# Holding back GpSimd's weight sums for the sixth and seventh output product of a Strassen-like layer

## The chip, the cores and the metric

One core of a Trainium2 chip. The metric is the device time of one execution in microseconds (us), median over runs. All runs quoted are in the fast state. Ratios are the mean time of one kernel's fast runs over that of the other's of the same rounds, so not quite the ratio of the medians quoted beside them.

## The reference, cut to what matters

```python
attn_out = _attn_ref(q, k, v, proj)          # hashed attention, 4 x 8 heads, 768 x 64
x = attn_out.transpose(0, 2, 1, 3).reshape(3072, 512)
h = x @ w_in                                 # 512 -> 2048
g = h * (1.0 / (1.0 + np.exp(-1.702 * h)))
return g @ w_out                             # 2048 -> 512: the part that matters here
```

## The kernel before

Both layers are computed with seven products in place of eight (a Strassen-like form with seven right-hand and left-hand sums), and in `g @ w_out` this is done twice, one form inside the other. So there are three blocks of tokens, each with seven *output products* (order `OUTER`), and each of these is made of seven *part products* on TensorE. An output product needs

- four sums of quarters of W_out (`inner_sums`), made on GpSimd (POOL) once, and used by all three blocks,
- four sums of quarters of g (`g_sums`: t1, a difference in place, t2, t4), made on VectorE for each output product during the one before it,
- additions of the part products on VectorE, and for some output products the accumulation onto an earlier one (`acc`).

In this kernel the operands lie in tiles of SBUF, and TensorE's products in tiles of PSUM.

```python
def sums_a(eng, a11, a12, s3, a22, s1, s2, s4, a21=None):
    a21 = s3 if a21 is None else a21
    return [lambda: eng.tensor_tensor(s1, a21, a22, op=Alu.add),
            lambda: eng.tensor_tensor(s3, a11, a21, op=Alu.subtract),
            lambda: eng.tensor_tensor(s2, s1, a11, op=Alu.subtract),
            lambda: eng.tensor_tensor(s4, a12, s2, op=Alu.subtract)]
# sums_b, used by g_sums on nc.vector: t1, b12 in place, t2, t4 (cut)
# ...
OUTER = (1, 2, 6, 7, 5, 3, 4)
# ...
def inner_sums(at):                  # at: place in OUTER; four sums of 128 x 512 on GpSimd
    # ... (at == 0 cut)
    return sums_a(nc.gpsimd, *w_quarters(OUTER[at])) if at < len(OUTER) else []
# ...
def product_of_halves(n, acc, after):
    # ... (cut)
    nc.scalar.copy(u, product(1))
    add(c11, product(2), u)
    if acc is not None:
        add(c11, c11, acc[:, 0])     # the accumulation of the first quarter
    nc.scalar.copy(c12, product(3))
    after(0)
    add(v, product(6), u)            # the fourth part product: the first that reads t2
    add(c21, product(7), v)
    if acc is not None:
        add(v, v, acc[:, 1])
        add(c22, c21, acc[:, 3])
        add(c21, c21, acc[:, 2])
    add(c12, c12, v)
    after(1)                         # t1 of the next output product
    # ... (product 5, after(2), product 4, after(3): the other g_sums of the next)
# ...
for n, (sb, o) in enumerate(steps_out):        # 21 output products
    # ... (fetch of the next g cut)
    for f in inner_sums(n + 4):                # GpSimd's sums for the fifth, sixth, seventh
        f()                                    # are issued in the first, second, third
    later_sums = g_sums(n + 1)
    # ... (cut)
    ms[o] = product_of_halves(n, None if acc is None else ms[acc], after)
```

The order on GpSimd is the order above, and nothing else makes these sums wait: GpSimd runs them as soon as it has done the work issued to it before, in the first layer (in the trace, from 642.6 us on).

Of the kernel before, what the change touches and what calls it, by code (L numbers as in the profile page):

```python
# [8 lines left out]
F32 = mybir.dt.float32  # L9
# [29 lines left out]
def kernel(  # L39
# [17 lines left out]
    nc = tc.nc  # L57
# [147 lines left out]
# [7 lines that stand above are left out]
# [458 lines left out]
    def feed_forward(tag, late=()):  # L670
# [8 lines left out]
        OUTER = (1, 2, 6, 7, 5, 3, 4)  # L679
        with ExitStack() as fctx:  # L680
# [62 lines left out]
            def w_quarters(o):  # L743

                w = wqs[LEFT[o]]
                x = [w[:, i, F4 * j : F4 * (j + 1), :] for i in range(2) for j in range(2)]
                at = OUTER.index(o)
                if at == 0:
                    return x[0:2] + rooms[3:4] + x[3:] + rooms[0:3]
                return x + rooms[3 * at + 1 : 3 * at + 4]  # L750

            def inner_sums(at):

                if at == 0:
                    w = w_quarters(OUTER[0])
                    return sums_a(nc.gpsimd, *w, wqs[LEFT[OUTER[0]]][:, 1, 0:F4, :])
                return sums_a(nc.gpsimd, *w_quarters(OUTER[at])) if at < len(OUTER) else []
# [4 lines left out]
            def fetch(n):  # L762
                sb, o = steps_out[n]
                for h in range(2):
                    cs = slice(h * F4, (h + 1) * F4)
                    loader[0].dma_start(out=raw_g[n % 2][:, cs], in_=g_dram[len(LEFT) * sb + RIGHT[o], :, cs, :])
# [14 lines left out]
            def g_sums(n):  # L781
                return sums_b(nc.vector, *g_quarters(n)) if n < len(steps_out) else [lambda: None] * 4
# [3 lines left out]
            def turned(c, i, j, q0, q1):  # L786

                for q in range(q0, q1):
                    h, k = divmod(q, 2)
                    y = ys[j].rearrange("p b (d r) -> p r b d", r=4)[:, 2 * i + h, k * (TH // 32) : (k + 1) * (TH // 32), :]  # L790
                    nc.vector.transpose(y, c[:, q].rearrange("p (b t) -> p b t", t=32))  # L791

            def written(sb, j, halves, queues):
                for b in halves:
                    blocks = slice(b * (TH // 32), (b + 1) * (TH // 32))
                    for a in range(4):
                        t0 = (2 * sb + j) * XT + b * TH
                        dst = out[t0 : t0 + TH, a * P : (a + 1) * P].rearrange("(b t) d -> t b d", t=32)
                        queues[a % len(queues)].dma_start(out=dst, in_=ys[j][32 * a : 32 * (a + 1), blocks, :])

            def product_of_halves(n, acc, after):

                sb, o = steps_out[n]
                wq, gq = w_quarters(o), g_quarters(n)
                m = wholes[n % len(wholes)]
                u, v = (gp.tile([P, TH], F32, tag=x, name=x, bufs=2) for x in ("u", "v"))
                c11, c12, c21, c22 = (m[:, i] for i in range(4))

                def product(i):
                    ps = bank()[:, 0:TH]  # L810
                    for c in range(F4):
                        nc.tensor.matmul(ps, wq[LEFT[i]][:, c, :], gq[RIGHT[i]][:, c, :], start=(c == 0), stop=(c == F4 - 1))  # L812
                    return ps

                def add(dst, x, y):
                    nc.vector.tensor_tensor(dst, x, y, op=Alu.add)  # L816
# [4 lines that stand above are left out]
                    add(c11, c11, acc[:, 0])  # L821
                nc.scalar.copy(c12, product(3))
                after(0)
                add(v, product(6), u)
# [6 lines that stand above are left out]
                after(1)  # L831
                p = product(5)
                add(c22, p, c21 if acc is None else c22)
                add(c12, p, c12)
                after(2)
                add(c21, product(4), c21)
                after(3)
                return m
# [14 lines left out]
            for sb in range(n1):  # L853
                for mt in range(MT):
                    n = sb * MT + mt
# [41 lines left out]
            st2 = fctx.enter_context(tc.tile_pool(name=f"st2{tag}", bufs=1, side="right"))  # L897
            ys.update({j: st2.tile([P, XT // 32, P], F32, name=f"y{j}") for j in range(2)})
            ms, pending = {}, []
            for n, (sb, o) in enumerate(steps_out):  # L900
                final = n + 1 == len(steps_out)
                if 0 < n and n + 1 < len(steps_out):
                    fetch(n + 1)
                for f in inner_sums(n + 4):
                    f()
                later_sums = g_sums(n + 1)
                m = wholes[n % len(wholes)]

                def after(at):
                    if at == 0:  # L910
                        while pending:
                            pending.pop(0)()

                    for f in later_sums[at : at + 1] if n == 0 else ([], later_sums[0:1], later_sums[1:2], later_sums[2:])[at]:
                        f()
                    if final and at == 2:
                        for q in (0, 1, 3):
                            turned(m, 1, 0, q, q + 1)
                        written(sb, 0, (1,), loader + [nc.scalar])
                    if final and at == 3:  # L920
                        turned(m, 1, 0, 2, 3)
                        written(sb, 0, (0,), loader + [nc.scalar])

                acc = {6: 1, 7: 6, 2: 1, 3: 6, 4: 7}.get(o)
                if o == 3:
                    pending.pop(0)()
                ms[o] = product_of_halves(n, None if acc is None else ms[acc], after)

                def flat(x):
                    return x.rearrange("p q t -> p (q t)")  # L930

                if o == 5:
                    m5, m6, m7 = (ms[i] for i in (5, 6, 7))
                    pending += [lambda a=m6, b=m5: nc.vector.tensor_tensor(flat(a), flat(a), flat(b), op=Alu.add),
                                lambda a=m5, b=m7: nc.vector.tensor_tensor(flat(a), flat(a), flat(b), op=Alu.add),
                                lambda a=m5: turned(a, 1, 1, 0, 4)]
                elif o in (2, 3):
                    pending.append(lambda a=ms[o], j=int(o == 3): turned(a, 0, j, 0, 4))
                    if o == 3:
                        pending.append(lambda sb=sb: written(sb, 1, (0, 1), loader))  # L940
                elif o == 4 and not final:
                    pending.append(lambda a=ms[4]: turned(a, 1, 0, 0, 4))
                    pending.append(lambda sb=sb: written(sb, 0, (0, 1), loader))
                yield

    def whole(steps):
        for _ in steps:
            pass

    ff = feed_forward("", in_chunks[len(in_chunks) - LATE :])  # L950
    attention(ff)
    whole(ff)
# [5 lines left out]
    with tc.If(unsafe, preferred_fallthrough_block=False):  # L958
        with tc.tile_pool(name="cv3", bufs=1) as cv:
            for x in in_chunks:  # L960
                whole(convert(cv, *x))
        for f in in_sums(0):
            f()
        shifted_attention()
        for f in sums_b(nc.vector, *quarters_x(0)):
            f()
        whole(feed_forward("2"))
# [27 lines left out]
```

## Time and profile before

| | kernel before |
|---|---|
| median of the first three runs | 895.95 us (895.92 to 897.0) |
| median of six runs, with those beside the changed kernel | 896.31 us |
| span of the profiled execution | 895.6 us, mean granted clock 0.993 |
| TensorE busy | 877.3 us (98%) |
| longest wait of TensorE | 3.8 us, for t2a in the third output product |
| that product, start to start | 19.07 us, where the fifth takes 12.09 |

(The granted clock is the share of TensorE's full clock that it was given; 1.00 is full.) Nearly all of the span TensorE is at work. A kernel like this is read by looking for the few places where it isn't: the list of TensorE's waits comes first, then the timeline of the engine that it waited for. The lines are in the prediction below.

### The profile page before, as it was taken

To read this page: it belongs to the slowest core of one execution; us is meant where nothing else is said; L and a number is where in the kernel's file an instruction comes from. 1 tells how busy PE (TensorE), PEld (TensorE's weight loads), DVE (VectorE), ACT (ScalarE), POOL (GpSimd) and SP (SyncE) were. 2 spreads that over 40 slices of the span, in tenths; PEclk is the share of its full clock that TensorE was granted. 3 is DMA by queue.
4 is the path that set the end of the run, shared out by engine and by line. 5 is a ranking of instruction groups with operands and counts; after the bars stand their busy time and mean duration, and the time that the engine had idled before them with its cause. 6 is when DMAs were issued, how large, how long until landed. Compare 5 with 4: busy or idle time off the path is not lost.

```text
span 895.6 us, 11963 instructions
## 1 busy us (share of the span) xinstructions
PE 877.3 (98%) x4077; PEld 507.2 (57%) x4077; DVE 710.9 (79%) x1020; ACT 313.3 (35%) x519; POOL 312.5 (35%) x273
## 2 busy tenths in 40 slices
PE   9999999999999999999999999999989999999995
PEld 5444444444444444444444444444868888888884
DVE  4598888888889954777777887888896977897785
ACT  5765666666665642223222222322000000000000
POOL 4243233222333263766433444659950000000000
PEclk9999999999999999999999999999989999999998
DMA  4644544556544103555456545575825565467524
GB/s 102 113 90 82 103 82 80 87 98 96 95 83 82 45 1 118 194 194 192 160 199 211 200 165 203 193 249 183 304 102 188 176 208 213 161 229 235 189 95 97
DMA packets 169477, 132.01 MB, mean 147 GB/s; under 512 B 123936, under 2 KB 138432, under 8 KB 164032
## 3 DMA queue, kind: packets, MB, share of 16 engines
q1 hardware_dynamic: 167712, 129.69, 50.7%
q10 hardware_dynamic: 1696, 1.48, 0.6%
q8 instruction: 34, 0.56, 0.3%
q14 instruction: 35, 0.29, 0.1%
HBM read 79.69 MB, written 50.33 MB: 145 GB/s over the span
## 4 chain that ended last, share of the span: by engine, by line
PE 94%; DVE 3%; DMA 1%; issue 1%; ACTq 0%; SPq 0%; ACT 0%; DVEq 0%
PE product L699 32%; PE product L812 27%; PE ps L429 16%; PE av L453 14%; PE dn L472 3%; PE hash L405 1%; DVE xT L816 1%; PE tp L363 1%; DMA q<-in_q_dram 1%; ACTq L417 0%; PE warm L356 0%; PE hash L370 0%; DVE y L791 0%; DVE acc L445 0%; DVE t2a L218 0%
## 5 line engine op out<-in xcount | busy, mean ns | idle before, releaser
L430 ACT ACTIVATE e<-ps 128x768 f32<-128x768 f32 x192 | 151.4, 812 | 19.2 <-PE ps L429 13.2
L429 PE MATMUL ps<-qT,kT 64*128 64x384 f32 x768 | 155.1, 482 | 0.0
L699 PE MATMUL product<-xT,w_in_sb 128*128 128x512 f32 x288 | 135.4, 592 | 0.0
L453 PE MATMUL av<-e,v 128*64 128x385 f32 x768 | 130.2, 486 | 0.9 <-ACT xT L466 0.9
L437 POOL TENSOR_TENSOR acc<-e 128x768 f32<-128x768 f32 x32 | 49.6, 1549 | 209.5 <-DVE acc L445 90.3
L707 ACT ACTIVATE c<-c 128x512 f32<-128x512 f32 x72 | 45.4, 630 | 186.6 <-issue 78.9
L453 PEld LDWEIGHTS av<-e,v 128*64 128x64 f32 x768 | 54.9, 136 | 70.6 <-issue 69.0
L699 PEld LDWEIGHTS product<-xT,w_in_sb 128*128 128x128 f32 x288 | 54.6, 190 | 68.5 <-issue 63.1
L699 PE MATMUL product<-t_x,s_in 128*128 128x512 f32 x192 | 90.2, 592 | 0.0
L429 PEld LDWEIGHTS ps<-qT,kT 64*128 64x128 f32 x768 | 68.2, 188 | 35.5 <-issue 35.5
L216 POOL TENSOR_TENSOR v<-c,u 128x512 f32<-128x512 f32 x24 | 34.1, 1422 | 129.4 <-ACT c L707 129.4
L818 ACT COPY u<-product 128x256 f32<-128x256 f32 x21 | 7.8, 372 | 173.4 <-PE product L812 131.8
L429 PE MATMUL ps<-qf,kf 64*128 64x384 bf16 x384 | 63.0, 324 | 0.7 <-ACT e L430 0.5
L699 PEld LDWEIGHTS product<-t_x,s_in 128*128 128x128 f32 x192 | 36.5, 190 | 45.9 <-issue 43.8
L438 POOL TENSOR_TENSOR acc<-acc,e 128x768 f32<-128x768 f32 x32 | 56.7, 1771 | 2.5
L699 PE MATMUL product<-xT,s_in 128*128 128x512 f32 x96 | 45.1, 592 | 0.0
L699 PE MATMUL product<-t_x,w_in_sb 128*128 128x512 f32 x96 | 45.1, 592 | 0.0
L429 PEld LDWEIGHTS <-kf 64*128 64x128 bf16 x384 | 18.9, 94 | 42.2 <-issue 20.7
L479 DVE STREAM_TRANSPOSE rt<-dn 128x384 f32<-128x384 f32 x32 | 18.6, 580 | 25.7 <-PE dn L472 25.6
L465 ACT COPY vs<-av 128x1 f32<-128x1 f32 x32 | 5.1, 159 | 95.1 <-PE av L453 95.0
L812 PE MATMUL product<-raw_g,xT 128*128 128x256 f32 x152 | 36.3, 388 | 0.0
L490 DVE TENSOR_TENSOR xT<-xT,rt 128x384 f32<-128x384 f32 x32 | 32.6, 1020 | 1.7
(200 smaller groups left out, 1569.6 us busy)
## 6 DMA issues: line engine op xcount, KB each, us to landing
raw_g<-g_dram SPq DMA_DIRECT2D x22, 1024.0 KB
s_in<-g_dram SPq DMA_DIRECT2D x20, 1024.0 KB
g_dram<-c SPq DMA_DIRECT2D x72, 256.0 KB
g_dram<-t SPq DMA_DIRECT2D x48, 256.0 KB
raw<-in_moe_w_out_dram SPq DMA_DIRECT2D x16, 512.0 KB
raw<-in_moe_w_in_dram SPq DMA_DIRECT2D x15, 512.0 KB
v<-in_v_dram SPq DMA_DIRECT2D x32, 192.0 KB
g_dram<-u SPq DMA_DIRECT2D x24, 256.0 KB
```

Source lines behind the costliest of these rows:

```text
L216: return [lambda: eng.tensor_tensor(t1, b12, b11, op=Alu.subtract), lambda: eng.tensor_tensor(b12, b22, b12, op=Alu.subtract), lambda: eng ...
L429: nc.tensor.matmul(ps[:, j, 0:HS], a[hs, keys], m[hs, cols], start=not last, stop=last)
L430: nc.scalar.activation(es[c][:, kt, :, 0:HS], ps[:, :, 0:HS], Act.Exp, scale=1.0 / D**0.5)
L437: nc.gpsimd.tensor_tensor(acc, es[c][:, 0, :, 0:HS], es[c][:, 1, :, 0:HS], op=Alu.add)
L438: nc.gpsimd.tensor_tensor(acc, acc, es[c][:, 2, :, 0:HS], op=Alu.add)
L453: nc.tensor.matmul(av[D * j : D * (j + 1), :], vt[:, t, j, :], es[c][:, t, j, :], start=(t == 0), stop=(t == T - 1))
L472: nc.tensor.matmul(dn[D * j : D * (j + 1), :], ones, acc[:, j, :], start=True, stop=True)
L479: nc.vector.transpose(rt, dn)
L490: nc.vector.tensor_tensor(x_of(n, c), x_of(n, c), rt.rearrange("p (t s) -> p t s", t=GT), op=Alu.mult)
L699: nc.tensor.matmul(ps, wq[LEFT[i]][:, kc, :], xq[RIGHT[i]][:, kc, :], start=(kc == 0), stop=(kc == K2 - 1))
L707: nc.scalar.activation(c, c, Act.Gelu_apprx_sigmoid)
L812: nc.tensor.matmul(ps, wq[LEFT[i]][:, c, :], gq[RIGHT[i]][:, c, :], start=(c == 0), stop=(c == F4 - 1))
```

## The change

In the kernel before, GpSimd's eight sums for the sixth and seventh output product run beside VectorE's sums in the second and third. They are not needed so early. In the changed kernel two copies of one element, each reading an element that VectorE writes, are put on GpSimd's queue ahead of them, so that they start later.

```diff
             ms, pending = {}, []
+            mark = st2.tile([1, 1], F32, name="mark")
             for n, (sb, o) in enumerate(steps_out):
                 ...
-                for f in inner_sums(n + 4):
+                if n in (3, 4):
+                    nc.gpsimd.tensor_copy(mark, ms[OUTER[n - 1]][0:1, 0, 0:1])
+                for f in inner_sums({0: 4, 3: 5, 4: 6}.get(n, len(OUTER))):
                     f()
```

`ms[OUTER[n - 1]][0:1, 0, 0:1]` is an element of c11 of the output product before. The copy waits for the last write to it, the accumulation `add(c11, c11, acc[:, 0])` of the third and of the fourth output product, which VectorE does about half way through them.

## The prediction

> **What bounds the kernel now.** I read the page first, then TensorE's waits over the whole run, then the timeline of TensorE, VectorE and GpSimd around the one long wait, then a table of stretches there. The page says that TensorE is nearly always busy (the first line below) and that GpSimd (POOL) has nothing to do after about three quarters of the span (the second, one digit per 22.4 us).
>
> ```profile
> PE 877.3 (98%) x4077; PEld 507.2 (57%) x4077; DVE 710.9 (79%) x1020; ACT 313.3 (35%) x519; POOL 312.5 (35%) x273
> ...
> POOL 4243233222333263766433444659950000000000
> ```
>
> So only a wait of TensorE can be worth anything. Its list of waits has five entries, and four are short. The longest is one wait for the sum t2a, in the second layer:
>
> ```profile
> PE product L812 <- DVE t2a L218: 3.8, 1, 3.8
> PE dn L472 <- DVE acc L445: 1.5, 1, 1.5
> ```
>
> I number the second layer's output products 1 to 7, in their order of execution; each is made of seven part products of 1.73 us, 12.08 us in all (from 667.85, the start of the fourth, to 679.93, that of the fifth). The wait stands in the third, before its fourth part, the first to read t2a. TensorE's timeline there, then the stretches (length, busy of PE, PEld, DVE, ACT, POOL, then the granted clock, DMA share and GB/s):
>
> ```profile
> 648.78 3.62 PE L812 MATMUL product<-raw_g,xT 128*128 128x256 f32 x16
> 652.23 1.89 PE L812 MATMUL product<-raw_g,w_in_sb 128*128 128x256 f32 x8
> 657.93 3.75 PE L812 MATMUL product<-t2a,w_in_sb 128*128 128x256 f32 x8 [3.81 <-DVE t2a L218]
> 661.48 3.08 PE L812 MATMUL product<-raw_g,xT 128*128 128x256 f32 x8
> 664.39 1.89 PE L812 MATMUL product<-t1a,w_in_sb 128*128 128x256 f32 x8
> ```
>
> ```profile
> 648.78:654.12 5.34, 5.34 (x25) 4.37 (x23) 5.34 (x6) 0.37 (x1) 5.18 (x4) 1.00 0.18 75
> 654.12:657.93 3.81, 0.00 (x1) 0.03 (x1) 3.78 (x4) 0.37 (x1) 3.73 (x3) 0.88 0.00 0
> 657.93:664.39 6.46, 6.46 (x16) 5.22 (x17) 5.62 (x8) 0.00 (x0) 4.53 (x3) 0.54 0.46 162
> 664.39:667.85 3.46, 3.46 (x18) 3.04 (x17) 3.19 (x7) 0.00 (x0) 0.00 (x0) 1.00 0.62 194
> ```
>
> The reader is to see two losses. TensorE idles 3.81 us, and then the granted clock is 0.54, so that the next two parts take 6.46 us in place of 3.45. Together: 648.78 to 667.85 is 19.07 us where 12.08 is normal, a loss of **6.99 us**. After 657.93 the chain that ended last is TensorE's work without a break up to 882, so what is saved here is saved at the end.
>
> Why t2a is late stands in VectorE's and GpSimd's lines. In the fourth product, with no GpSimd work, a 1024-column sum takes 1.22 us and two 256-column sums of SBUF operands 0.88. In the second and third they take this long:
>
> ```profile
> 646.87 2.89 DVE L816 TENSOR_TENSOR xT<-xT 128x256 f32<-128x256 f32 x2
> 649.68 1.48 DVE L816 TENSOR_TENSOR xT<-xT,v 128x256 f32<-128x256 f32 x1
> 651.09 2.28 DVE L216 TENSOR_TENSOR t1a<-raw_g 128x1024 f32<-128x1024 f32 x1
> 653.96 1.62 DVE L217 TENSOR_TENSOR raw_g<-raw_g 128x1024 f32<-128x1024 f32 x1
> 655.84 1.95 DVE L218 TENSOR_TENSOR t2a<-raw_g,t1a 128x1024 f32<-128x1024 f32 x1
> ```
>
> ```profile
> 648.03 1.45 POOL L208 TENSOR_TENSOR w_in_sb<-xT 128x512 f32<-128x512 f32 x1
> 649.55 1.33 POOL L209 TENSOR_TENSOR xT<-xT 128x512 f32<-128x512 f32 x1
> 650.84 1.44 POOL L210 TENSOR_TENSOR w_in_sb<-w_in_sb,xT 128x512 f32<-128x512 f32 x1
> 652.37 2.13 POOL L211 TENSOR_TENSOR w_in_sb<-xT,w_in_sb 128x512 f32<-128x512 f32 x1
> 654.46 2.24 POOL L208 TENSOR_TENSOR w_in_sb<-w_out_sb 128x512 f32<-128x512 f32 x1
> ```
>
> These five GpSimd sums are four for the sixth product and the first of four for the seventh: work needed only at about 685 and 697, done at the worst place.
>
> [...] GpSimd's sum of 650.84 ends at 652.28, and t1a, issued at 651.09, ends at 653.37, 1.09 later; GpSimd's sum of 652.37 then ends at 654.50, 1.13 later. So an operation that finds the other engine at work ends about 1.1 us (512 columns on GpSimd, 1024 on VectorE) or 0.28 us (256 on VectorE) after the other's end. [...] sums whose other operand is a product in PSUM do stay at 0.41 us here, and transposes at 2.01 for four against 2.04 later. [...] 0.5 from about 657.5 after an idle time from 654.12; after the 1.51 us wait at 44 to 46 us it stayed 1.00.
>
> **The change part by part.** It leaves the four GpSimd sums for the fifth product where they are (642.63 to 648.07). It holds the four for the sixth behind a one-element copy, which by the built program waits for one VectorE operation: the accumulation of the first quarter of the third product. It holds the four for the seventh behind the same accumulation of the fourth product. Removed: nothing. Added: two copies of one element on GpSimd, off the path. VectorE's order and TensorE's stay the same.
>
> *Third product.* GpSimd falls silent at 648.07. VectorE's first sum of the pair from 646.87 still ends at 648.36 as now. From there on the fourth product's lines give an uncontended pace: end of that sum (677.92, half the pair 677.48 + 0.88) to the end of t2a (681.88 + 1.22 = 683.10) is 5.18 us. So t2a ends at 648.36 + 5.18 = 653.54. TensorE starts 0.14 us after it (now: 657.79 to 657.93), at 653.68; its turn comes at 648.78 + 5.18 = 653.96. The wait goes with 0.28 us to spare, and with it the clock drop: **-6.99 us**.
>
> *First release.* t4g follows t2a to 654.8, then the sum of the first quarter and its accumulation to 655.6. There GpSimd starts, from about 656.0, within the third product. Four transposes to 657.6 do not contend; its first sum ends at 657.3, the second at 658.6. VectorE's next SBUF sums come after part five, at 658.1: it waits to 658.6 and ends at 658.9; then they alternate, GpSimd to 660.0, VectorE to 660.3, GpSimd to 661.4, VectorE to 661.7. Without GpSimd that third sum ends at 648.78 + 10.51 = 659.29 (678.36 less 667.85). Delay: 2.4 us. The slack from there to the fourth product's t2b: uncontended it ends 15.25 us after the product's start (683.10 - 667.85), and may end 12.08 + 5.18 - 0.14 = 17.12 after it, so 1.87 us. Left: a new wait of about **+0.5 us** before the fourth part of the fourth product.
>
> *Second release.* In the fourth product the same accumulation ends at about 668.4, and GpSimd's sums for the seventh start at 668.7. The same alternation, now from 670.6, gives VectorE's third sum at 674.4 against 671.8 without: 2.6 us, less the slack of 1.87: **+0.7 us** in the fifth product. The fifth has no accumulations (8.3 us of VectorE work in 12), so nothing is handed on; the GpSimd sums are ready some 10 us and more before their products.
>
> Sum: -6.99 + 0.5 + 0.7 = -5.8; 895.95 - 5.8 = 890.2.
>
> **The rivals.** (a) *Clean gain*: the releases fall so that GpSimd blocks less than the slack; 889.0. For it: the delay depends on the phase, between about 1.1 and 3 us, and part lies below 1.87. Against it: GpSimd's four sums last over 5 us and begin only 2 us before VectorE's four accumulations. (b) *The wait moves on*: the released sums delay t2b or t2a by more, up to 1.2 us in each product: 891.4. [...] (c) *The wait stays*: the 0.28 us to spare is an estimate, and a miss by 1 us would leave 1 us of wait, without the clock drop; 891. (d) GpSimd becomes the bound at the sixth or seventh product: against it, over 10 us of room.
>
> **Range and chances.** From 889.0 with no new wait to about 891.4 with two large ones, and runs of one kernel scatter by 1.1 us (895.92 to 897.0): 888.7 to 892.3. A gain over 2% would be 17.9 us, more than all waits of TensorE together; a loss over 2% has no mechanism. Hence 0.01 faster, 0.98 same, 0.01 slower.
>
> **What would show each step right or wrong.** Right: TensorE's 3.8 us wait for t2a gone, granted clock 1.00 throughout 648 to 668, t1a and t2a at 1.22 us; GpSimd silent from 648.1 to about 656; VectorE's accumulations at 658 to 662 and 670 to 675 stretched; two waits of TensorE under 1.3 us for t2b and t2a. Wrong: [...] GpSimd's sums released elsewhere than by the two accumulations; a third product longer than 12.5 us.

## The result, and the profile after

| | before | after |
|---|---|---|
| median us of six runs each | 896.31 (895.52 to 897.0) | 891.35 (890.56 to 891.88) |
| ratio of the fast runs | | 0.9944, 95% interval 0.9931 to 0.9957 |
| mean granted clock, profiled execution | 0.993 | 0.996 |
| span from the first part product of `g @ w_out` to the end | 895.6 - 624.61 = 270.99 us | 888.7 - 623.37 = 265.33 us |
| third output product, start to start | 19.07 us | 659.67 - 647.54 = 12.13 us |

The changed kernel is 0.56% faster (5.0 us): a gain well under 2%, as predicted. The last two rows compare the one execution of each that was profiled: 5.66 us of the difference of their spans lie behind the start of `g @ w_out`. (The 1.24 us before it lie in work that the change doesn't touch.)

TensorE's waits after the change. The 3.8 us are gone; two short waits in the same line of the kernel are new (0.4 us each is the time with no matmul at work; what they cost is read from the start times further down):

```profile
PE dn L472 <- DVE acc L445: 1.5, 1, 1.5
...
PE product L812 <- ACT xT L822: 0.4, 1, 0.4
PE product L812 <- ACT t_x L822: 0.4, 1, 0.4
```

TensorE's timeline after the change, the third and fourth part of the third, fourth and fifth output product. In the third they follow each other by 1.72 us, without a wait; in the fourth by 2.34 and in the fifth by 2.30, so 0.61 and 0.57 us more than the 1.73 of an undisturbed part:

```profile
651.00 1.89 PE L812 MATMUL product<-raw_g,w_in_sb 128*128 128x256 f32 x8
652.72 1.93 PE L812 MATMUL product<-t2a,w_in_sb 128*128 128x256 f32 x8
...
663.12 1.89 PE L812 MATMUL product<-s_in,w_in_sb 128*128 128x256 f32 x8
665.46 1.97 PE L812 MATMUL product<-t2b,w_in_sb 128*128 128x256 f32 x8 [0.45 <-ACT xT L822]
...
675.89 1.89 PE L812 MATMUL product<-raw_g,w_in_sb 128*128 128x256 f32 x8
678.19 1.97 PE L812 MATMUL product<-t2a,w_in_sb 128*128 128x256 f32 x8 [0.41 <-ACT t_x L822]
```

VectorE after the change: t1a and t2a of the third product at their undisturbed 1.22 us (before: 2.28 and 1.95), but the two accumulations within the third product at 2.90 us in place of 0.88, and then t2b, which ends at 665.36, 0.1 us ahead of TensorE's start at 665.46:

```profile
648.06 1.22 DVE L216 TENSOR_TENSOR t1a<-raw_g 128x1024 f32<-128x1024 f32 x1
...
651.32 1.22 DVE L218 TENSOR_TENSOR t2a<-raw_g,t1a 128x1024 f32<-128x1024 f32 x1
...
657.72 2.90 DVE L816 TENSOR_TENSOR xT<-xT 128x256 f32<-128x256 f32 x2
...
664.15 1.21 DVE L218 TENSOR_TENSOR t2b<-s_in,t1b 128x1024 f32<-128x1024 f32 x1
```

GpSimd after the change: silent for 7.60 us, then the copy and, at once, the sums for the sixth product, the last two beside the accumulations above:

```profile
654.66 0.17 POOL L907 COPY mark<-xT 1x1 f32<-1x1 f32 x1 [7.60 <-DVE xT L816]
654.80 1.28 POOL L208 TENSOR_TENSOR w_in_sb<-xT 128x512 f32<-128x512 f32 x1
656.16 1.27 POOL L209 TENSOR_TENSOR xT<-xT 128x512 f32<-128x512 f32 x1
657.38 1.55 POOL L210 TENSOR_TENSOR w_in_sb<-w_in_sb,xT 128x512 f32<-128x512 f32 x1
659.01 1.33 POOL L211 TENSOR_TENSOR w_in_sb<-xT,w_in_sb 128x512 f32<-128x512 f32 x1
```

The granted clock was 1.00 in every stretch from 648 to 700 us of this execution. So the picture is the predicted one: the wait and the clock drop gone, two small waits left. What is still argued and not shown: that the left waits are GpSimd's doing (the profile names ScalarE's copies as their releasers), that reading SBUF is how GpSimd disturbs VectorE, and that a wait below some length is free of the clock drop.

### The profile page after: what moved, and what is told of

Same layout as the page of the kernel before. It is cut to its first block, busy times and chain, and to the rows that moved or that the text cites. A ratio compares the mean times of both kernels' runs of the same rounds, so it can differ in the third digit from the quotient of the medians.

```text
span 888.7 us, 11969 instructions
## 1 busy us (share of the span) xinstructions
PE 873.2 (98%) x4077; PEld 503.5 (57%) x4077; DVE 709.3 (80%) x1020; ACT 313.9 (35%) x519; POOL 309.7 (35%) x275
## 4 chain that ended last, share of the span: by engine, by line
PE 96%; DVE 2%; DMA 1%; ACTq 0%; issue 0%; SPq 0%; ACT 0%; DVEq 0%
PE product L699 32%; PE product L812 28%; PE ps L429 16%; PE av L453 14%; PE dn L472 3%; PE hash L405 1%; DMA q<-in_q_dram 1%; PE tp L363 0%; ACTq L417 0%; DVE xT L816 0%; PE warm L356 0%; PE hash L370 0%; DVE y L791 0%; DVE acc L445 0%; SPq L325 0%
```

## The experiments

Theory A: a GpSimd sum that reads SBUF and a VectorE sum with two SBUF operands exclude each other (in the traces t1a took 2.28 us with GpSimd at work and 1.22 with it silent); the wait before, and the two waits after, are that alone, plus the clock. Theory B: the two waits after come from VectorE's own load or from ScalarE's copies; GpSimd's work costs in another way (its mere activity, its order against TensorE). The first four kernels ran on one chip beside 19 runs of the kernel before (median 896.38 us, 893.56 to 897.58), the next four on another beside 28 runs of it (895.9 us, 894.31 to 898.09).

### The changed kernel again

> The changed kernel again, unaltered, for comparison on one chip with the next three. Both theories: 5.0 to 5.8 us below the kernel before, two waits of TensorE of about 0.6 us each (before the fourth part of the fourth and of the fifth output product).

No edit. 891.22 us (890.83 to 891.72, five runs), ratio 0.9946: 4.8 us below the kernel before (5.2 by the medians; 5.0 to 5.8 were expected). The waits showed as 0.6 and 0.4 us in the list. It is the reference for the next three.

### Release after t2

```diff
-                    nc.gpsimd.tensor_copy(mark, ms[OUTER[n - 1]][0:1, 0, 0:1])
+                    nc.gpsimd.tensor_copy(mark, g_tiles[n][1][0:1, 0, 0:1])
```

The copies now read t2 of the fourth and of the fifth output product, so that each group of sums starts some 9 us later, behind the operand for which TensorE waited.

> The same two holds, but each copy reads the second sum (t2) of the product's own right-hand side, so that GpSimd's sums start after the operand that TensorE waits for, not before the accumulations. Theory A [...]: both waits of 0.6 us vanish, 1.2 us below the changed kernel, 6.2 to 7.0 below the kernel before; accumulations of 256 columns back at 0.42 us each. Theory B (they come from VectorE's own load in products with accumulations, or from ScalarE's copy, which the profile names as releaser): both waits stay at about 0.6 us, and the time is that of the changed kernel.

889.92 us (889.54 to 890.53), ratio 0.9934, output correct: 1.3 us below the changed kernel in the same rounds, and 5.9 below the kernel before (6.5 by the medians; 6.2 to 7.0 were expected). Neither product wait is left in TensorE's list. TensorE's third and fourth part of the fourth product in this kernel, 1.73 us apart:

```profile
663.50 1.89 PE L812 MATMUL product<-s_in,w_in_sb 128*128 128x256 f32 x8
665.23 1.89 PE L812 MATMUL product<-t2b,w_in_sb 128*128 128x256 f32 x8
```

VectorE's two accumulations of the third product, back at the undisturbed time, and GpSimd, which is silent there:

```profile
657.86 0.87 DVE L816 TENSOR_TENSOR xT<-xT 128x256 f32<-128x256 f32 x2
```

```profile
663.53 1.23 POOL L907 COPY mark<-t2b 1x1 f32<-1x1 f32 x1 [16.29 <-DVE t2b L218]
664.73 1.26 POOL L208 TENSOR_TENSOR w_in_sb<-xT 128x512 f32<-128x512 f32 x1
```

ScalarE's copies were not touched, so Theory B's releaser falls: the profile had named the engine that ended last, not the one waited for. The start times say so too: here the fourth part starts at 665.23, before ScalarE's copy begins at 665.43, so it doesn't need that copy. GpSimd and VectorE still meet in this kernel (a VectorE accumulation from 665.09 takes 1.18 us in place of 0.43), but no wait of TensorE follows from it. Note the copy of one element: 0.17 us in the changed kernel, 1.23 here, because it comes just as VectorE starts t4 (663.50, 1.23 us). So a copy of one element waited for the whole of VectorE's sum; the second copy, at 675.84, took 1.23 us as well, beside the next t4.

### Without the sums for the sixth and seventh

```diff
-                for f in inner_sums({0: 4, 3: 5, 4: 6}.get(n, len(OUTER))):
+                for f in inner_sums({0: 4}.get(n, len(OUTER))):
```

(The copies are left out as well. The result is wrong on purpose.)

> Wrong result on purpose: the eight GpSimd sums for the sixth and seventh product are left out. It is the most that any place for them can give. Theory A: no wait for the second layer's products, 7.0 us below the kernel before, equal to the release after t2 within 0.5 us. Theory B: the waits of 0.6 us stay here too.

889.89 us (888.98 to 889.99), ratio 0.9932: the release after t2 (889.92) has all that there is to get. No product wait. The expected 7.0 us below the kernel before were 6.1 by the ratio and 6.5 by the medians. The likely reason (only one execution of the kernel before was traced): what the kernel before loses differs from execution to execution, and the profiled one, at 897.43 us, was among its slow ones.

### Only the seventh product's sums held

```diff
-                if n in (3, 4):
+                if n == 4:
                     nc.gpsimd.tensor_copy(mark, ms[OUTER[n - 1]][0:1, 0, 0:1])
-                for f in inner_sums({0: 4, 3: 5, 4: 6}.get(n, len(OUTER))):
+                for f in inner_sums({0: 4, 1: 5, 4: 6}.get(n, len(OUTER))):
```

> Only the seventh product's sums are held; the sixth's stand where they stood before. Theory A with the clock as a second cost: GpSimd is silent from about 654.5 us of the old timeline, so t2a of the third product ends about 1.1 us earlier than before: a wait of about 2.7 us (before: 3.8)[...]; plus a wait of about 0.6 us in the fifth product: 889.0 + 2.7 + 0.6, that is 3.5 to 4 us below the kernel before. If the clock drop came from something other than the length of the idle time, it stays: only 0.5 us below the kernel before.

894.85 us, but from 892.89 to 897.24 in 14 runs; ratio 0.9985. That is 1.3 us below the kernel before (1.5 by the medians), where 3.5 to 4 were expected: a miss. The wait was shorter than before, 3.30 us, but 0.6 longer than expected. Of that, 0.2 us differs from run to run (the sum ahead of the accumulations took 1.18 us in this execution and 0.96 in the one I worked from); the rest was a wrong estimate, as the seventh product's sums had stretched only t2a itself (1.95 in place of 1.22 us, so 0.7 and not 1.1 to be gained). The wait of 0.6 us expected in the fifth product didn't show: there two accumulations took 1.95 us, not 2.89, and the slack took that up. And the clock fell all the same in the profiled execution. TensorE's timeline, then stretches of 1 us (the third figure from the end is the granted clock): the idle time begins at 654.18, and the clock falls before 657 (by the mean of 0.89 at about 656.8, 2.6 us after):

```profile
657.48 3.75 PE L812 MATMUL product<-t2a,w_in_sb 128*128 128x256 f32 x8 [3.30 <-DVE t2a L218]
```

```profile
655.00:656.00 1.00, 0.00 (x0) 0.00 (x0) 1.00 (x2) 0.00 (x0) 0.00 (x0) 1.00 0.00 0
656.00:657.00 1.00, 0.00 (x0) 0.00 (x0) 1.00 (x2) 0.00 (x0) 0.00 (x0) 0.89 0.00 0
657.00:658.00 1.00, 0.52 (x1) 0.50 (x2) 0.96 (x2) 0.00 (x0) 0.00 (x0) 0.50 0.00 0
```

The three fastest of the 14 runs (892.89 to 893.17) had a mean clock of 0.996, as most runs of the kernels without a wait; the seven from 894.37 to 895.56 had 0.994, the four of 895.8 and above 0.993. So it seems that in some executions the drop comes and in others not, and not always for as long. That the 2.7 us expected here would be too short for the drop was an assumption of mine, not shown by a trace; the 3.30 us measured were enough, as the 3.81 us had been in the kernel before. The last two experiments look at that.

### GpSimd writes, and doesn't read

```diff
+                if n in (1, 2):
+                    s1, s2, s4 = w_quarters(OUTER[n + 4])[4:7]
+                    for x in (s1, s2, s4, s1, s2, s4, s1, s2):
+                        nc.gpsimd.memset(x, 0.0)
-                for f in inner_sums({0: 4, 3: 5, 4: 6}.get(n, len(OUTER))):
+                for f in inner_sums({0: 4}.get(n, len(OUTER))):
```

(The copies are left out as well.)

> Wrong result on purpose: at the places where the kernel before has the GpSimd sums for the sixth and seventh product, GpSimd writes zeros to the same tiles, sixteen times 128 x 512, and reads nothing from SBUF. Theory A [...]: VectorE's sums beside them stay at 0.42 and 1.22 us, the third product has no wait, and the time is that without the sums (6 us below the kernel before). Rival: it is GpSimd's mere work beside VectorE, or its order against TensorE, that costs; then the sums stretch, and a wait of up to 3.8 us stands in the third product.

890.39 us (890.2 to 890.48), ratio 0.9934, the result wrong as intended. GpSimd wrote zeros from 647.64 to 655.15. VectorE's sums beside it, t1a and t2a of the third product, were undisturbed, and no product wait was left:

```profile
647.64 4.25 POOL L909 MEMSET w_in_sb<- 128x512 f32 x9
```

```profile
648.69 1.22 DVE L216 TENSOR_TENSOR t1a<-raw_g 128x1024 f32<-128x1024 f32 x1
...
651.96 1.22 DVE L218 TENSOR_TENSOR t2a<-raw_g,t1a 128x1024 f32<-128x1024 f32 x1
```

So it is not GpSimd's mere work at this place, nor that it writes these tiles. Two differences remain between a memset and a sum, the reads of SBUF and the arithmetic. The one-element copy above points to the reads: it does no arithmetic and took 1.23 us, though there it was GpSimd that waited. No run here has arithmetic without reads, so which of the two it is was not shown.

### One hold for both groups

```diff
-                if n in (3, 4):
+                if n == 3:
```

> The change with its second hold taken away: the sums for the sixth and the seventh follow one another from the accumulation of the third product on. Theory A, by alternation of the two engines: from the accumulations on, every SBUF sum of VectorE up to t2b of the fourth product waits for one of GpSimd's; t2b ends about 3.9 us late, a wait of about 4 us before the fourth part of the fourth product and the clock halved for some us after it: the time of the kernel before (895 to 897.5). If one hold is enough: 891 to 892.

896.42 us (895.39 to 897.21, 12 runs), ratio 1.0003: the gain is gone. The wait, in the fourth product now, is 3.94 us where the alternation worked out by hand gave about 4, and the granted clock was 0.50 from 669 to 674 us after it:

```profile
668.82 3.75 PE L812 MATMUL product<-t2b,w_in_sb 128*128 128x256 f32 x8 [3.94 <-issue]
```

```profile
662.76 2.28 DVE L216 TENSOR_TENSOR t1b<-s_in 128x1024 f32<-128x1024 f32 x1
```

t1b has the 2.28 us that t1a had before. The change works by its second hold as much as by its first: holding eight sums together only moves the same collision on by one product. (The releaser is given as "issue" here; t2b ended at 668.72, 0.1 us ahead of TensorE's start.)

### A wait made on purpose, of 2 and of 3 us

Both start from the release after t2.

```diff
 # in g_sums, for the third output product, ahead of t2 (x: the quarters and t tiles)
+                        for _ in range(2):
+                            nc.vector.tensor_tensor(x[6], x[3], x[3], op=Alu.add)
 # the second kernel also
+                        nc.vector.tensor_tensor(x[6][:, 0:2], x[3][:, 0:2], x[3][:, 0:2], op=Alu.add)
```

> The kernel that releases after t2, with a wait made on purpose: two more VectorE sums of 1.22 us (into the tile of t4, overwritten after) before t2a of the third product, 0.3 us of slack there, so a wait of about 2.2 us of TensorE with nothing of GpSimd beside it. If a wait shorter than about 2.7 us costs its own length alone: 2.2 us more than that kernel (about 892.1), clock 1.00 after it. If each wait of over 2 us costs clock: up to 5 us more.

> The same with one half-size sum more (about 0.65 us): a wait of about 2.9 us. Expected: in some runs its own length alone (about 892.8), in some with the clock halved for 6 us after it (about 896), as the run with only the seventh product's sums held scattered (892.9 to 897.2 with a wait of 3.3 us).

The waits were 2.19 and 2.92 us. TensorE's line of the first kernel, then of the second:

```profile
656.11 3.05 PE L822 MATMUL product<-t2a,w_in_sb 128*128 128x256 f32 x8 [2.19 <-DVE t2a L218]
```

```profile
655.69 1.97 PE L823 MATMUL product<-t2a,w_in_sb 128*128 128x256 f32 x8 [2.92 <-DVE t2a L218]
```

The shorter wait is the one after which the eight matmuls took 3.05 us: the granted clock was 0.50 from 657 to 660 us in that execution. After the longer one it stayed 1.00. In stretches of 1 us, for the first kernel:

```profile
656.00:657.00 1.00, 0.89 (x4) 0.84 (x5) 1.00 (x1) 0.00 (x0) 0.00 (x0) 0.92 0.00 0
657.00:658.00 1.00, 1.00 (x4) 0.82 (x3) 0.97 (x4) 0.00 (x0) 0.00 (x0) 0.50 0.00 0
```

The mean of 0.92 puts the fall at about 656.8, when TensorE had been back at work for 0.7 us. In finer stretches the halved clock lasted 3.4 us here, but 6.8 us in the kernel before and with one hold for both groups. So a drop can cost more or less, which fits the groups of run times.

Over the runs: with 2.19 us, four runs at 891.98 to 892.16 us (mean clock 0.996) and two at 894.36 and 894.79 (0.994), median 892.14 as expected for the wait alone; with 2.92 us, seven runs from 892.42 to 893.4 and eight from 894.37 to 896.39, median 894.37. (The two kernels ran on the second chip and the release after t2 on the first; the kernel before differed by 0.5 us between them.)

So whether the clock falls differs from execution to execution, and it falls more often after a longer wait: by the run times in two of six at 2.19 us, eight of 15 at 2.92, eleven of 14 at 3.30 (the seventh product's hold alone). At 3.8 us, in the kernel before, it is nearly always: the fastest of its 47 runs here, 893.56 us with a mean clock of 0.998, is the only one with a mean clock above 0.995. The trend holds over all four; the first two alone are too few runs to tell apart. One execution of each kernel was traced, and the others are sorted by their times, as if their waits were the same. What decides it in one execution these runs do not show.

## Why the prediction was right

Predicted 890.2 us (888.7 to 892.3), measured 891.35: in the range, and the step's parts one by one:

- *The third product's wait goes.* Right. t2a was predicted to end 4.76 us after the product's start and ended at 5.00 (652.54 - 647.54); TensorE's turn was at 5.18. The predicted margin of 0.28 us was under 0.1 in fact (TensorE starts some 0.1 us after t2), so rival (c) came close: that no wait at all was left in the traced executions is in part luck.
- *First release.* Right. GpSimd's sums were to start 7.2 us after the third product's start, and did at 7.26; VectorE's third accumulating sum was to end at 12.9 us and ended at 13.08 (660.62 - 647.54). New wait 0.5 us predicted, 0.61 measured. The two undo-experiments show its cause: it is gone when GpSimd is released behind t2, and gone without the sums.
- *Second release.* Right in place and cause; 0.7 us predicted, 0.57 measured.
- *The rivals.* By the time alone (b), 891.4, and (c), 891, fit better than the 890.2 predicted; what decides for the prediction's account is the trace, with no wait in the third product and one each in the fourth and fifth. The clean gain (a) was not what the change got, but what the release after t2 got: 889.92. Rival (b) in a worse form, a wait that moves on and brings the clock drop back (3.94 us, then a clock of 0.50), is what one hold for both groups did. Rival (d) didn't appear.
- *The sum.* In the two profiled executions it is -5.66 us from the start of `g @ w_out` on, against -5.8 predicted. By the runs it is -5.0. The term that was mis-sized is the first, "a loss of 6.99 us": it was read in one execution, of 897.43 us, and taken from a median of 895.95. Without the sums the gain is 6.1 us by the ratio (6.5 by the medians), probably because the clock drop is part of the loss and differs from run to run.
- *What was wrong.* I took it that a wait clearly shorter than the one traced leaves the clock alone. That was an assumption: the trace had one wait with the drop (3.81 us) and one without (1.51 us), and showed nothing of the lengths between. A wait of 2.19 us brought it back, in two runs of six by their times, one of them traced. The prediction had also read its own trace a little late: it has the clock at 0.5 "from about 657.5", 3.4 us after the idle time began at 654.12, and finer stretches show the fall at about 657.05, 2.9 us after. The prediction of the time didn't hang on it, as the waits left were 0.6 us, but the expectation for the seventh product's hold alone did, and failed.

What carried the whole estimate, that GpSimd's sums and VectorE's sums of SBUF operands hold each other up, agrees with the numbers looked at here: a VectorE sum of 1024 columns beside GpSimd's sums takes 1.62 to 2.28 us in place of 1.22; beside memsets it keeps its 1.22. Where both engines had work waiting they alternated, one operation each, so that a sum of 256 columns that takes 0.42 us alone took about 1.45 (2.90 for two).

## What to carry to other kernels

Work that is off the critical path still costs if it slows the engine that feeds it (here t1a took 2.28 us beside GpSimd's sums and 1.22 without). Before moving GpSimd work "later", work out which of VectorE's sums of two SBUF operands it will then meet (those with one operand in PSUM stayed at 0.41 to 0.42 us), and how much slack stands between them and the next operand. Here the better place to release it was just behind that operand, not at the next handy write; that took the gain from 5 to 6 us with one changed operand. And read a loss off several runs if a clock drop is part of it.
